# Where the feed-forward stands in the first 18 steps of a top-k attention kernel

## The chip, the cores and the metric

The kernel runs on one core of a Trainium2 chip. A core has TensorE (PE in the profile, with its weight loads as PEld), VectorE (DVE), ScalarE (ACT), GpSimd (POOL) and SyncE (SP), which here issues most of the transfers. Each engine works through its own list of instructions, and they meet through semaphores. The metric is the device time of one execution in microseconds, as the median of several; less is better.

## What is computed

Attention in which each query keeps its 32 largest scores, followed by a feed-forward block with the activation h - tanh(h). The two weight matrices lie in memory as float64, and the kernel converts them; q, k, v and all arithmetic are float32.

```python
B, H, S, D = 8, 8, 576, 64            # q, k, v
scores = np.matmul(q, k.transpose(0, 1, 3, 2)) / np.sqrt(D)
kth = np.partition(scores, -32, axis=-1)[..., -32:-31]
scores = np.where(scores >= kth, scores, -1e9)
attn = np.exp(scores - scores.max(-1, keepdims=True))
attn = attn / (attn.sum(-1, keepdims=True) + 1e-9)
x = (attn @ v).transpose(0, 2, 1, 3).reshape(B * S, H * D)     # 4608 x 512
h = x @ w_in                                                   # 512 x 2048
out = (h - np.tanh(h)) @ w_out                                 # 2048 x 512
```

## The kernel before

The work is a software pipeline over steps. A step is 128 queries of two heads (or the remaining 64 queries of four heads). While step n is searched for its 32 largest values, step n+1 is multiplied, step n-1 is masked and put through the exponential, and step n-2 is turned and multiplied with the values. In the 18 steps of the first batch (`pe` is true) the turning is done by PE, as transposes against an identity, later by DVE and transfers. In the same early steps the 32 pieces of the weights are converted from float64 by DVE, ACT and POOL, two to four pieces a step in steps 0 to 10.

The loop gives each engine its instructions in the order in which they stand here:

```python
for n in range(-4, NS + 4):
    pe = here(-2) and steps[n - 2].pe
    ...
    share, usable = rate(), converted[0]
    if pe:
        w = turn_pe(n - 2)
        next(w)                      # 8 of 9 transposes, 2 copies by ACT
    if here(-1):
        mask(n - 1, exact)           # ACT, POOL
    if here(0):
        search(n, exact, between)    # DVE; the conversion of weights lies in between()
    ...
    if pe:
        spread(n - 2)                # POOL: rx, the divisors
    deal(0.4)
    if here(1):
        scores(n + 1)                # PE, then one copy by ACT
    if pe:
        next(w)                      # the last transpose and its copy
    if here(-1):
        expo(n - 1)                  # ACT
    deal(0.2)
    if pe and steps[n - 2].last:
        values(n - 2)                # PE, ACT, POOL
    deal(0.2)
    for fn in todo.pop(n, []):
        fn()                         # loads
    deal(0.2)
```

`deal` takes items of the feed-forward from a list. A unit of 128 or 256 tokens is put on that list when its last values are done; the first one is, at n = 5. `rate` spreads what is on the list, and what is coming, evenly over the steps.

```python
def deal(part):
    nonlocal credit
    credit += part * share
    while work and credit > 0 and work[0][0] <= usable:
        work.pop(0)[2]()
        credit -= 1
    credit = min(credit, 1.0)
```

An item is one of two things: `ffn_h`, a part of x @ w_in into the tile `hps`, and for every second item a `tanh` and a copy by ACT and a subtraction by POOL; or `ffn_o`, two matmuls of the product with w_out into the tile `ops`, with a copy by ACT after the last part of eight. The profile records each of these float32 matmuls as two instructions.

The functions that the steps speak of, shortened:

```python
def scores(n):
    ps = sc_ps.tile([P, 2, 2, 512], FP32, tag="sc", name="scps")     # one buffer
    ...                                                              # L237: matmuls
    sc = scpool.tile([P, 2, 2, S2], FP32, tag="sc", name="sc")
    nc.scalar.copy(sc[:], ps[:, :, :, 0:S2])                         # L245

def search(n, exact, between):
    ...
    nc.vector.tensor_tensor(lo, ps[:, :, 0, 0:S2], sc[:, :, 1, :], ALU.min)   # L267
    nc.vector.tensor_tensor(hi, ps[:, :, 0, 0:S2], sc[:, :, 1, :], ALU.max)   # L268
    ...                                                              # L270, L275, L278

def mask(n, exact):
    ...                                                              # POOL: tb, nb
    for t in range(2):
        nc.scalar.activation(zv[:, t, :], scf[:, t, :], AF.Relu, ...)          # L307
        nc.gpsimd.tensor_tensor(zv[:, t, :], scf[:, t, :], zv[:, t, :], ALU.subtract)  # L310

def turn_pe(n):
    ...
    for k0 in range(0, KC, J):                                       # KC = 9, J = 4
        zt = zt_ps.tile([P, 512], FP32, tag="zt", name="zt")         # two buffers
        for k in range(kn):
            nc.tensor.transpose(zt[:, ...], z[:, ...], ident[:])     # L409
        nc.scalar.copy(et[:, k0 : k0 + kn], zt[:, ...])              # L412
        if k0:
            yield

def values(n):
    av = zt_ps.tile([P, 2, N], FP32, tag="zt", name="av")            # the same two buffers
    ...                                                              # L433: matmuls of et and v
    nc.tensor.transpose(av[:, 1, ...], rx[:, i], ident[:])           # L441
    nc.scalar.copy(xs[:, :, 0:w], av[:, :, 0:w])                     # L445
    nc.gpsimd.tensor_tensor(xt(u)[...], xv[:, 0], xv[:, 1], ALU.mult)  # L457
    if n in done:
        work.extend(ffn(u))

def convert(piece, slot):                                            # three parts
    ...                                                              # L157, L163: DVE
    nc.scalar.activation(f[:], fu, AF.Relu, bias=e1151[:], scale=-(2.0**23))   # L158
    nc.scalar.activation(e.bitcast(I32), f[:], AF.Relu, bias=e255[:], scale=-1.0)  # L161
    nc.scalar.activation(dst, dst.bitcast(U32), AF.Copy, bias=1.0, scale=2.0**-28) # L166
    yield
    nc.vector.scalar_tensor_tensor(out=fu, in0=hi, ...)              # L169
    nc.gpsimd.tensor_tensor(dst, dst, f[:], ALU.mult)                # L172
```

Of the kernel before, what the change touches and what calls it, by code (L numbers as in the profile page):

```python
# [48 lines left out]
def kernel(  # L49
# [198 lines left out]
    def search(n, exact, between):  # L248

        x = st[n]
        sc, ps = x["sc"], x.pop("ps")
        m = x["m"] = mpool.tile([P, 2, TOP], FP32, tag="m", name="m")
        ab = abpool.tile([P, 2, S + 8], FP32, tag="ab", name="ab")
        if exact:
            cur = [sc[:, t].rearrange("p s k -> p (s k)") for t in range(2)]
            nxt = [ab[:, t, 0:S] for t in range(2)]  # L260
            last = nxt
        else:
            x["ab"] = ab
            cur = nxt = [ab[:, t, 0:S2] for t in range(2)]
            last = [ab[:, t, 0 : S2 + 8] for t in range(2)]
            hi, lo = ab[:, :, 0:S2], ab[:, :, S2 + 8 :]
# [3 lines that stand above are left out]
                nc.vector.max(ab[:, t, S2 : S2 + 8], lo[:, t, :])  # L270
        rounds = TOP // 8
        for i in range(rounds):
            m8 = slice(8 * i, 8 * i + 8)
            for t in range(2):
                nc.vector.max(m[:, t, m8], last[t] if i == rounds - 1 else cur[t])  # L275
            if i < rounds - 1:
                for t in range(2):
                    nc.vector.match_replace(nxt[t], m[:, t, m8], cur[t], NEG)  # L278
                cur = nxt
            between(i)  # L280
# [3 lines left out]
    def mask(n, exact):  # L284

        x = st[n]
        sc, m = x["sc"], x.pop("m")
        scf = sc[:].rearrange("p t s k -> p t (s k)")
        tb = mpool.tile([P, 2], FP32, tag="tb", name="tb")
        if exact:  # L290
            nc.gpsimd.tensor_scalar(tb[:], m[:, :, TOP - 1], BIG, None, ALU.mult)
        else:
            for t in range(2):
                nc.gpsimd.tensor_scalar(  # L294
                    tb[:, t : t + 1],
                    m[:, t, TOP - 1 : TOP],
                    m[:, t, TOP - 9 : TOP - 8],
                    BIG,
                    ALU.min,
                    ALU.mult,  # L300
                )
        nb = mpool.tile([P, 2], FP32, tag="nb", name="nb")
        nc.gpsimd.tensor_scalar(nb[:], m[:, :, 0], -scale, None, ALU.mult)
        z = zpool.tile([P, 2 * S], FP32, tag="z", name="z")
        zv = z[:].rearrange("p (t k) -> p t k", t=2)
        for t in range(2):
            nc.scalar.activation(  # L307
                zv[:, t, :], scf[:, t, :], AF.Relu, bias=tb[:, t : t + 1], scale=-BIG
            )
            nc.gpsimd.tensor_tensor(zv[:, t, :], scf[:, t, :], zv[:, t, :], ALU.subtract)  # L310
        if not exact:
            ab = x.pop("ab")
            for t in range(2):
                nc.gpsimd.tensor_scalar(  # L314
                    bad[:, t, n : n + 1],
                    ab[:, t, S2 + 7 : S2 + 8],
                    BIG,
                    tb[:, t : t + 1],
                    ALU.mult,
                    ALU.is_gt,  # L320
                )
        x.update(z=z, zv=zv, nb=nb)
# [26 lines left out]
    def spread(n):  # L349

        if steps[n].last:
            rd = rds.pop(n)
            nq = steps[n].nq
            rx = rxs[n] = xpool.tile([P, 2, 2, D], FP32, tag="rx", name="rx")
            nc.gpsimd.tensor_copy(
                rx[:, 0:nq], rd[:, 0:nq].unsqueeze(3).to_broadcast([P, nq, 2, D])
            )
# [23 lines left out]
    def spread_keys(n):  # L381


        zx = zxs.pop(n)
        rem = steps[n].rem
        et = ets[n] = et_rem if rem else etpool.tile([P, 4 * S], FP32, tag="et", name="et")
        w = steps[n].nq * S // 2
        for a in range(NG):
            for c in range(NG):
                nc.sync.dma_start(  # L390
                    et[group(c), a * w : (a + 1) * w], zx[group(a), c * w : (c + 1) * w]
                )

    def turn_pe(n):

        g, z = steps[n], st.pop(n)["z"]
        if g.rem:
            et = et_rem
        elif g.i:
            et = ets.pop(n - 1)  # L400
        else:
            et = etpool.tile([P, 4 * S], FP32, tag="et", name="et")[:]
        ets[n] = et
        et = tiles(et, g.nq)[:, :, :, g.i, :].rearrange("p a k j -> p k a j")
        for k0 in range(0, KC, J):
            kn = min(J, KC - k0)
            zt = zt_ps.tile([P, 512], FP32, tag="zt", name="zt")
            for k in range(kn):
                nc.tensor.transpose(  # L409
                    zt[:, k * P : (k + 1) * P], z[:, (k0 + k) * P : (k0 + k + 1) * P], ident[:]  # L410
                )
            nc.scalar.copy(  # L412
                et[:, k0 : k0 + kn],
                zt[:, 0 : kn * P].rearrange("p (k a j) -> p k a j", a=NG, j=G),
            )
            if k0:
                yield
# [152 lines left out]
    def run(exact):  # L570
# [67 lines left out]
        def here(i):  # L638
            return 0 <= n + i < NS

        def between(i):
            for fn in at_round.pop((n, i), []):
                fn()
            if i == 0 and here(-2):
                invert(n - 2)
                if not steps[n - 2].pe:
                    turn_z(n - 2)
# [16 lines left out]
        def rate():  # L664


            have, low, high = len(work), 0.0, None
            coming = sorted((t, u.n // 8) for u, t in ready.items() if t > n)
            for t, k in coming + [(NS + 4, 0)]:
                r = have / max(t - n, 1)  # L670
                high = r if high is None else min(high, r)
                have += k
            for u, t in begun.items():
                if t > n and u in before:
                    need = [i + 1 for i, x in enumerate(work) if x[1] is before[u]]
                    if need:
                        low = max(low, need[-1] / (t - n))
            return max(low, high)
# [3 lines left out]
# [10 lines that stand above are left out]
            if here(-3) and not steps[n - 3].pe:  # L692
                spread(n - 3)
            for m in (n - 4, n - 3):
                if 0 <= m < NS and steps[m].last and steps[m].lag == n - m:
                    values(m)
# [3 lines that stand above are left out]
                next(w)  # L700
            if here(-1):
                mask(n - 1, exact)
            if here(0):
                search(n, exact, between)
            elif here(-2):
                between(0)
            if here(-2) and not pe and steps[n - 2].last:
                spread_keys(n - 2)
            if pe:
                spread(n - 2)  # L710
            deal(0.4)
            if here(1):
                scores(n + 1)
            if pe:
                next(w)
            if here(-1):
                expo(n - 1)
            deal(0.2)
            if pe and steps[n - 2].last:
                values(n - 2)  # L720
            deal(0.2)
            for fn in todo.pop(n, []):
                fn()
            deal(0.2)
# [4 lines left out]
    with tc.manual_schedule():  # L729
        run(False)  # L730
# [10 lines left out]
    with tc.If(again > 0):  # L741
        with tc.manual_schedule():
            run(True)
# [29 lines left out]
```

## Time and profile before

| | before |
|---|---|
| time, median of 3 runs | 1548.89 us (1547.83 to 1551.28) |
| span of the profiled run | 1548.3 us, 25298 instructions |
| PE busy | 1440.6 us, 93% |
| DVE busy | 1347.3 us, 87% |
| POOL busy | 941.5 us, 61% |
| ACT busy | 883.4 us, 57% |
| shares of the chain that ended last | PE 73%, DVE 9%, others 5% or less each |

The busy share is a mean over the whole span, and the kernel has parts with different limits; so the page is read with the forty slices beside the totals, and then the trace by step. A busy PE is a modelled thing, as the ends of matmuls are. In the list of waits a line names who waited, for whom, how long in total, how often and the longest. A releaser in brackets behind an instruction is who ended the idle time before it. A row of the timeline merges like instructions that follow each other.

Two waits stand large over the whole span and have to do with the steady part, not with the first 18 steps: in 300 to 1500 us ScalarE waits 147.7 us for the values of PE at line 445, and GpSimd 146.4 us for ScalarE at line 457. In that stretch PE is busy 99 to 100% from 400 us on, so they cost nothing there.

### The profile page before, as it was taken

The page shows a single profiled execution, that of the slowest core. Times are in us where ns is not written, and L with a number is a line of the kernel's source. Part 1 is how long each engine was busy: PE and PEld are TensorE (multiplying, and loading weights), DVE is VectorE, ACT ScalarE, POOL GpSimd, SP SyncE. Part 2 cuts the span into 40 slices and gives each one's busy share as a digit, 9 for nine tenths or more (in the row PEclk, how much of TensorE's full clock was granted, in tenths as well). Part 3 has the DMA queues.
Part 4 walks back from the last instruction along what each step waited for, and adds up shares of the span by engine and source line. Part 5 has one row for each costly group of instructions (what it writes and reads, how often), then busy time and mean ns, then how long its engine had stood idle before and what let it go on. Part 6 is the DMA issues. An engine that isn't in the chain of part 4 may idle for free.

```text
span 1548.3 us, 25298 instructions
## 1 busy us (share of the span) xinstructions
PE 1440.6 (93%) x7428; PEld 912.4 (59%) x7428; DVE 1347.3 (87%) x3828; ACT 883.4 (57%) x1567; POOL 941.5 (61%) x1525
## 2 busy tenths in 40 slices
PE   2467899999999999999999999999999999999997
PEld 1355466556565665656566665656566665656673
DVE  6997889999999999999999999999999999997300
ACT  4886767556565565656565565656565565655320
POOL 2776567667565675757575675757565675746420
PEclk9787899999999999999999999999999999999999
DMA  9954113334443354234433354234443345322200
GB/s 233 364 182 155 50 25 66 85 77 88 112 92 76 82 105 104 70 77 96 106 88 78 81 107 102 70 79 97 101 90 80 80 99 110 81 64 59 73 10 16
DMA packets 258835, 147.42 MB, mean 95 GB/s; under 512 B 210048, under 2 KB 217216, under 8 KB 258688
## 3 DMA queue, kind: packets, MB, share of 16 engines
q1 hardware_dynamic: 256912, 145.49, 38.6%
q8 instruction: 62, 1.02, 0.3%
q14 instruction: 85, 0.70, 0.2%
q10 hardware_dynamic: 1776, 0.22, 0.1%
HBM read 61.85 MB, written 9.44 MB: 46 GB/s over the span
## 4 chain that ended last, share of the span: by engine, by line
PE 73%; DVE 9%; SPq 5%; ACT 4%; DMA 3%; issue 3%; POOL 2%; DVEq 0%; ACTq 0%; POOLq 0%
PE hps L486 27%; PE ops L507 27%; PE av L433 9%; PE scps L237 8%; SPq L390 4%; DVE ab L278 3%; DVE m L275 3%; PE av L441 2%; SPq L200 1%; DMA zx<-in_moe_w_in_dram 1%; DVE spare L376 1%; DVE ab L270 1%; DVE ab L267 1%; DVE ab L268 1%; ACT sc L245 1%
## 5 line engine op out<-in xcount | busy, mean ns | idle before, releaser
L507 PE MATMUL ops<-w_out,g 128*128 128x512 f32 x1152 | 524.1, 601 | 0.0
L486 PE MATMUL hps<-xT,w_in 128*128 128x256 f32 (+1 forms) x2176 | 473.8, 373 | 1.2 <-POOL xT L457 1.2
L275 DVE MAX8 m<-ab 128x8 f32<-128x288 f32 (+1 forms) x1152 | 463.4, 443 | 0.0
L310 POOL TENSOR_TENSOR z<-sc,z 128x576 f32<-128x576 f32 x288 | 400.1, 1411 | 82.3 <-ACT z L307 82.3
L486 PEld LDWEIGHTS hps<-xT,w_in 128*128 128x128 f32 x2176 | 392.4, 193 | 73.4 <-issue 24.4
L278 DVE MATCH_REPLACE8 ab<-m,ab 128x288 f32<-128x288 f32 x864 | 375.5, 442 | 0.0
L507 PEld LDWEIGHTS ops<-w_out,g 128*128 128x128 f32 x1152 | 211.4, 191 | 243.0 <-issue 239.4
L307 ACT ACTIVATE z<-sc,tb 128x576 f32<-128x576 f32 x288 | 207.6, 769 | 154.0 <-POOL tb L294 154.0
L500 POOL TENSOR_TENSOR g<-g,th 128x512 f32<-128x512 f32 x144 | 184.0, 1278 | 123.0 <-ACT g L499 112.9
L245 ACT COPY sc<-scps 128x1152 f32<-128x1152 f32 x144 | 161.0, 1118 | 114.3 <-PE scps L237 110.4
L330 ACT ACTIVATE z<-z,nb 128x576 f32<-128x576 f32 x288 | 221.5, 773 | 7.1 <-POOL z L310 7.0
L237 PE MATMUL scps<-kT,qT 64*128 64x288 f32 (+1 forms) x1280 | 184.5, 437 | 30.7 <-DVE qT L222 28.5
L433 PE MATMUL av<-et,vb 128*64 128x256 f32 (+1 forms) x1088 | 132.9, 379 | 43.8 <-ACT et L412 37.7
L237 PEld LDWEIGHTS scps<-kT,qT 64*128 64x128 f32 (+1 forms) x1280 | 100.1, 181 | 122.9 <-issue 60.0
L267 DVE TENSOR_TENSOR ab<-scps,sc 128x576 f32<-128x576 f32 x144 | 107.6, 747 | 70.1 <-POOL bad L314 58.2
L498 ACT ACTIVATE th<-hps 128x512 f32<-128x512 f32 x144 | 85.4, 593 | 107.8 <-PE hps L486 105.4
L457 POOL TENSOR_TENSOR xT<-xs 128x256 f32<-128x256 f32 (+1 forms) x68 | 47.3, 695 | 160.7 <-ACT xs L445 160.6
L445 ACT COPY xs<-av 128x512 f32<-128x512 f32 (+1 forms) x84 | 44.2, 526 | 163.6 <-PE av L441 163.4
L433 PEld LDWEIGHTS av<-et,vb 128*64 128x64 f32 x1088 | 75.5, 139 | 102.9 <-ACT et L412 39.6
L340 POOL TENSOR_SCALAR rd<-den 128x2 f32<-128x2 f32 x144 | 33.4, 232 | 145.4 <-ACT z L330 100.3
L270 DVE MAX8 ab<-ab 128x8 f32<-128x288 f32 x288 | 116.4, 445 | 0.0
L268 DVE TENSOR_TENSOR ab<-scps,sc 128x576 f32<-128x576 f32 x144 | 107.4, 746 | 0.0
(67 smaller groups left out, 1249.0 us busy)
## 6 DMA issues: line engine op xcount, KB each, us to landing
et<-spare SPq DMA_DIRECT2D x448, 72.0 KB, 2.0
et<-zx SPq DMA_DIRECT2D x448, 72.0 KB, 2.0
kin<-in_k_dram SPq DMA_DIRECT2D x116, 72.0 KB, 2.3
vb<-in_v_dram SPq DMA_DIRECT2D x64, 128.0 KB, 2.5
out_dram<-ot SPq DMA_DIRECT2D x32, 256.0 KB, 2.2
qin<-in_q_dram SPq DMA_DIRECT2D x113, 72.0 KB, 2.3
w_out<-in_moe_w_in_dram SPq DMA_DIRECT2D x10, 512.0 KB, 5.7
w_out<-in_moe_w_in_dram SPq DMA_DIRECT2D x10, 511.5 KB, 6.3
```

The lines of the kernel that those rows point to most:

```text
L237: nc.tensor.matmul(ps[rows, t, s, 0:S2], qT[g.b, g.hp + i][half(t), qs], kT[g.b, g.hp + i][half(t), ks], start=True, stop=True,)
L245: nc.scalar.copy(sc[:], ps[:, :, :, 0:S2])
L270: nc.vector.max(ab[:, t, S2 : S2 + 8], lo[:, t, :])
L275: nc.vector.max(m[:, t, m8], last[t] if i == rounds - 1 else cur[t])
L278: nc.vector.match_replace(nxt[t], m[:, t, m8], cur[t], NEG)
L307: nc.scalar.activation(zv[:, t, :], scf[:, t, :], AF.Relu, bias=tb[:, t : t + 1], scale=-BIG)
L310: nc.gpsimd.tensor_tensor(zv[:, t, :], scf[:, t, :], zv[:, t, :], ALU.subtract)
L330: nc.scalar.activation(x["zv"][:, t, :], x["zv"][:, t, :], AF.Exp, bias=x["nb"][:, t : t + 1], scale=scale, accum_out=den[:, t : t + 1],)
L433: nc.tensor.matmul(av[half(t), 0, cols], vb[g.b, hp][:, t, c, :] if c < J else vr[g.b, hp][:, t, :], es[:, :, (J + 1) * t + c if c < J els ...
L486: nc.tensor.matmul(cur[u][:, s : s + w], w_in[j][:, c, fo : fo + P], u.xT[:, c, 0:w], start=(c == 0), stop=(c == CD - 1),)
L500: nc.gpsimd.tensor_tensor(g, g, th[:], ALU.subtract)
L507: nc.tensor.matmul(cur[u][:], u.g[o // 1024][:, o % 1024 // 512, o % 512 : o % 512 + P], w_out[f // FJ][:, f % FJ, :], start=(f == 0), sto ...
```

## The change

In a step in which PE does the turning, nothing of the feed-forward is dealt ahead of the scores any more; four fifths of the step's share are dealt between the last transpose and the values, and one fifth at the end of the step. The other steps deal as before. It is meant to give the next step's scores to ScalarE and VectorE sooner and to give PE work where the values wait for the copy of the last transpose.

```diff
             if pe:
                 spread(n - 2)
-            deal(0.4)
+            deal(0.0 if pe else 0.4)
             if here(1):
                 scores(n + 1)
             if pe:
                 next(w)
             if here(-1):
                 expo(n - 1)
-            deal(0.2)
+            deal(0.8 if pe else 0.2)
             if pe and steps[n - 2].last:
                 values(n - 2)
-            deal(0.2)
+            deal(0.0 if pe else 0.2)
             for fn in todo.pop(n, []):
                 fn()
             deal(0.2)
```

## The prediction

> **What bounds the kernel now.** I read the slices of the page first, to see where TensorE (PE) is not full. These are its lines for PE, VectorE (DVE) and the granted clock, 38.7 us to a digit:
>
> ```profile
> PE   2467899999999999999999999999999999999997
> ...
> DVE  6997889999999999999999999999999999997300
> ...
> PEclk9787899999999999999999999999999999999999
> ```
>
> From the sixth slice on PE is full and sets the end; only the first five or six slices leave it idle, at a lower clock. Those are the first 18 steps, the ones that the change touches. PE's whole work is the same before and after, so the change can only pay by making this head shorter. What it gains there should reach the end, because everything after the head is the same list of work.
>
> Second, the busy time by step. I took the start of the line 267 minimum as the start of a step. Steps 6 to 10 and, for contrast, step 12 (columns: stretch, length, then busy us of PE, weight loads, DVE, ScalarE (ACT), GpSimd (POOL), clock, DMA):
>
> ```profile
> 88.04:101.02 12.98, 11.11 (x76) 9.49 (x76) 12.85 (x35) 11.94 (x24) 9.42 (x13) 0.78 0.27 95
> 101.02:115.59 14.57, 7.23 (x64) 6.26 (x64) 12.88 (x36) 12.19 (x24) 11.71 (x15) 0.95 0.62 214
> 115.59:131.76 16.17, 12.00 (x86) 10.64 (x86) 12.85 (x34) 12.01 (x24) 12.15 (x15) 0.82 0.40 135
> 131.76:148.89 17.13, 11.14 (x63) 8.66 (x64) 12.75 (x35) 12.81 (x25) 12.06 (x15) 0.70 0.49 172
> 148.89:169.47 20.58, 12.26 (x38) 5.71 (x35) 14.22 (x37) 12.92 (x24) 10.96 (x14) 0.75 0.30 103
> ...
> 177.88:186.98 9.10, 9.10 (x55) 5.70 (x51) 7.61 (x25) 6.99 (x15) 5.07 (x9) 1.00 0.14 39
> ```
>
> Step 6 is as long as its DVE work (12.85 of 12.98). Steps 7 to 10 have nearly the same DVE work, but take 14.57 to 20.58 us: here nothing is full, so a chain across engines sets the pace. From step 12 PE is full. Steps 2 to 5 (37.46 to 88.04) have no feed-forward yet, and cannot change.
>
> Third, the timeline of PE in step 8, to find that chain (start, duration, line, form, idle before it and its releaser):
>
> ```profile
> 115.97 0.42 PE L433 MATMUL av<-et,vb 128*64 128x128 f32 x1
> 117.36 3.62 PE L486 MATMUL hps<-xT,w_in 128*128 128x128 f32 x16
> 120.78 1.18 PE L409 MATMUL zt<-ident,z 128*128 128x128 f32 x8
> 121.79 1.95 PE L486 MATMUL hps<-xT,w_in 128*128 128x128 f32 x16
> 123.67 1.24 PE L237 MATMUL scps<-kT,qT 64*128 64x288 f32 x8
> 125.01 1.95 PE L486 MATMUL hps<-xT,w_in 128*128 128x128 f32 x16
> 131.88 0.48 PE L433 MATMUL av<-et,vb 128*64 128x128 f32 x1 [3.90 <-ACT et L412]
> ```
>
> The reader is to see a loop. PE stands 3.90 us in the values for the last `et` copy (line 412) of ACT. Released, it first does one feed-forward item, cold (3.62 us), and only then the transposes (120.78) for which ACT stands in turn:
>
> ```profile
> 121.61 1.07 ACT L412 COPY et<-zt 128x512 f32<-128x512 f32 x2 [3.63 <-PE zt L409]
> 122.57 1.45 ACT L307 ACTIVATE z<-sc,tb 128x576 f32<-128x576 f32 x2
> 123.91 0.72 ACT L158 ACTIVATE f<-f,e 128x512 f32<-128x512 uint32 x1
> ...
> 129.59 0.58 ACT L498 ACTIVATE th<-hps 128x512 f32<-128x512 f32 x1
> 130.07 0.57 ACT L499 COPY g<-hps 128x512 f32<-128x512 f32 x1
> 130.53 1.13 ACT L245 COPY sc<-scps 128x1152 f32<-128x1152 f32 x1
> 131.54 0.29 ACT L412 COPY et<-zt 128x128 f32<-128x128 f32 x1
> ```
>
> ACT has 10.2 us of its own in order (121.61 to 131.83) before it releases PE. PE's part, 131.88 to ACT's next copies at 138.22 in the same timeline, is about 6.3. Sum 16.5; the step took 16.17, and the copies came 16.61 apart (121.61 to 138.22): this is the loop. DVE stands inside it, at the weight conversion. The waits of 90 to 200 us say the same:
>
> ```profile
> PE av L433 <- ACT et L412: 16.9, 4, 5.7
> DVE f L169 <- ACT f L161: 14.3, 4, 5.3
> ACT et L412 <- PE zt L409: 12.7, 9, 3.9
> ```
>
> **What the Trainium skill says.** "TensorE: Matmul & The Clock Gate", Part 1: after an idle window of about 3.4 us the clock falls to half. The trace agrees: the same 16 matmuls take 1.95 us in a run of work and 3.62 us after waits of 5.69 and 3.90. "Perfetto Trace Analysis", Tensor Engine Instruction: ACT and DVE take their queues strictly in order, and PE reorders only weight loads. The timeline agrees: at 115.37 ACT's 0.28 us `et` copy comes after nine conversion operations, a `tanh` and two copies, although its transpose was ready at 109. So where work stands in program order is what counts here, and that is all the change alters. The same page, Optimization Strategy, says that the most-contended engine may change between regimes; the step table shows it (DVE, then the loop, then PE).
>
> **The change part by part.** No instruction is removed or added. The shares dealt per step sum to 1.0 before and after, and the rule takes items until the credit is used, so each step deals as many items as before. From the code I get a share of about 2.4 items a step from step 6 to 18; the PE timeline shows 3, 2, 3, 2, 3 in steps 6 to 10. An item is 16 recorded matmuls of line 486 or 4 of line 507, 1.9 us warm. Before, usually one item stood ahead of the scores, none or one behind the last transpose, and one after the values. After: following the credit by hand (0.8 of 2.4 is 1.9 a step), two items stand between the last transpose and the values in each step, and a third after the values only in steps 6, 8, 10, 13, 15 and so on; none ahead of the scores.
>
> What this does to the loop:
> 1. **Ahead of the scores**, ACT's `tanh` and copy leave the path to the score copy: 130.53 minus 129.59 is 0.94 us. ACT's part falls from 10.2 to 9.3 us. They move to after the exponentials, where ACT had idle time.
> 2. **Before the values**, two items of 1.95 us, partly cold, fill the wait of 3.9 to 5.7 us. They should end before the `et` copy is there, so they cost nothing.
> 3. **After the values**, the item goes in two steps of three or every second one: 3.62 us less before the transposes. Where one stays, it is likely warm, 1.95.
> PE's part is then about 1.2 us of values, 0.3 of transposes of the divisors and 0.9 of transposes, 2.4, or 4.4 with an item. But ACT itself has two exponentials (1.95 us with their sums, 131.70 to 133.35 in the same timeline), `tanh` and copy (about 1.05) and `xs` (0.37), together 3.4, before its next copies. The loop is 9.3 plus 3.4 to 4.5, or **12.7 to 13.8 us**. DVE's own 12.75 to 12.88 then bounds or nearly bounds.
>
> By step:
> - Step 6 stays 12.98, DVE being full. Its third item still follows the values, so step 7 starts its transposes as late as before (104.75) and keeps its DVE wait of 1.49; it gains about 0.2.
> - Step 8: 16.17 to 13.0 (12.85 of DVE and a small wait), gain 3.2.
> - Step 9: its transposes follow an item, DVE waits some 0.7: 17.13 to 13.5, gain 3.6.
> - Step 10 converts four pieces: 14.22 of DVE, plus the DMA waits that the DVE timeline shows (0.28 and 0.74; a landing of a reused buffer, which don't move), plus 0.4: 15.6 instead of 20.58, gain 5.0.
> Sum 12.0. From step 11 PE is full and its work is the same. There are 1.3 and 0.24 us of idle PE in steps 14 and 15 (9.20 of 10.50, 9.14 of 9.38), and a cold item in step 11 (3.62 for 1.88, but some other work will be cold in its stead). Scores that come one item sooner help DVE, which is full from 214 us. I put 1.4 us for all that. Total 13.4: 1548.9 minus 13.4 is **1535.5 us**.
>
> **The rivals.** First, the head is bound by DVE, and then nothing comes of it. For: DVE is 85 to 99% busy there in most steps. Against: its waits in steps 7 to 10 sum to 14.3 on line 169 alone. Time then: 1547 to 1549. Second, a new wait takes the place of the old one: scores that stand directly behind the transposes meet a score buffer that DVE has not yet read (one buffer), the last transpose meets a `zt` buffer (two) that ACT has not copied, or the two items run cold (7.2 us) and delay the values. In step 8 the transposes would end near 118.3 and DVE has read the scores by 117; two cold items would still end about when the `et` copy comes. So I expect small waits, not the old ones; if the rival is right half the gain goes, 1541 to 1544. Third, the head gets shorter and it is lost again in the full part, as DVE is full from 214 to 400 us and PE from there. Both start sooner with the same lists, so I see no cause; time then about 1548. Fourth, the gain is larger: all DVE waits of steps 7 to 10 (68.45 us of steps against 52.7 of DVE work, so 15.75) and some 3 us of PE waits go, 1530.
>
> **Range and chances.** The fourth rival gives the lower end, 1529.5; half of my gain, with a little for the 3.5 us spread of the runs before, the upper end, 1543.5. Faster by over 2% needs 31 us, which isn't idle in this stretch: 0.01. A loss of 31 us would need a new wait of 2 us in every changed step: 0.01. Within 2%: 0.98, most of it on the faster side.
>
> **What would show it.** In the changed kernel: steps 8, 9 and 10 at about 13, 13.5 and 15.6 us with DVE work unchanged; `PE av <- ACT et` from 16.9 to some 6 us in total; `DVE f <- ACT f` from 14.3 to under 4; the 3.62 us cold items after the values gone; step 11 starting near 157.5 instead of 169.5 and the step at 214.4 near 201; the same PE work after. It would be wrong if PE waits at the scores for DVE's reading, if ACT's `tanh` and copies now delay `xs` and with it the second half of the transposes by more than the item that went, or if the head's gain is not found at the end.

## The result, and the profile after

The changed kernel takes **1544.22 us** (median of 6 runs, 1542.66 to 1545.55) where the kernel before takes 1549.22 (6 runs). The ratio is 0.9963, with a 95% interval of 0.995 to 0.9975: 5.0 us less, clear of the spread, but not the 13.4 us of the prediction, and 0.7 us above its range. The slices of the page, for PE, DVE and the granted clock, hardly differ from those of before:

```profile
PE   2567899999999999999999999999999999999997
...
DVE  6998899999999999999999999999999999997300
...
PEclk9887999999999999999999999999999999999999
```

The gain is all in the head. Step 6 begins 0.38 us sooner than before (87.66 to 88.04; the steps before it have the same work in both), step 11 4.85 us sooner (164.62 to 169.47), step 16 5.52 us sooner (208.92 to 214.44). From there to the end both traces take the same: 1333.88 us after, 1333.86 before. So what the head gains is kept, and the question is only why steps 7 to 10 gave 4.47 us (68.45 to 63.98) instead of the expected 12.0. The busy time by step, after, for steps 6 to 10 (columns as in the prediction):

```profile
87.66:100.64 12.98, 10.72 (x76) 8.64 (x76) 12.86 (x34) 11.93 (x24) 9.42 (x13) 0.81 0.30 93
100.64:116.57 15.93, 11.24 (x86) 10.05 (x86) 12.80 (x36) 11.91 (x23) 11.65 (x14) 0.89 0.56 198
116.57:130.34 13.77, 10.21 (x71) 8.21 (x70) 12.83 (x35) 12.21 (x24) 11.66 (x14) 0.75 0.43 148
130.34:147.74 17.40, 11.93 (x62) 8.67 (x62) 12.78 (x35) 13.06 (x26) 12.11 (x15) 0.79 0.49 177
147.74:164.62 16.88, 10.41 (x34) 5.42 (x31) 14.14 (x37) 12.76 (x24) 10.96 (x14) 0.80 0.36 126
```

Steps 8 and 10 got shorter (16.17 to 13.77, 20.58 to 16.88); steps 7 and 9 got longer (14.57 to 15.93, 17.13 to 17.40). DVE's work is what it was. Steps 7 and 9 are the ones that follow a step with an item behind the values. PE's timeline from the values of step 7 to the transposes of step 9 shows both kinds:

```profile
115.98 0.32 PE L433 MATMUL av<-et,vb 128*64 128x128 f32 x1 [2.92 <-ACT et L412]
...
118.35 0.47 PE L441 MATMUL av<-ident,rx 128*128 128x128 f32 x1 [1.70 <-POOL rx L355]
118.61 1.91 PE L409 MATMUL zt<-ident,z 128*128 128x128 f32 x8
120.46 2.29 PE L237 MATMUL scps<-kT,qT 64*128 64x288 f32 x8
122.68 0.47 PE L409 MATMUL zt<-ident,z 128*128 128x128 f32 x1
122.95 3.91 PE L486 MATMUL hps<-xT,w_in 128*128 128x128 f32 x32
...
129.74 0.32 PE L433 MATMUL av<-et,vb 128*64 128x128 f32 x1 [1.86 <-ACT et L412]
...
132.10 0.48 PE L441 MATMUL av<-ident,rx 128*128 128x128 f32 x1 [1.59 <-POOL rx L355]
132.37 3.62 PE L486 MATMUL hps<-xT,w_in 128*128 128x128 f32 x16
135.79 1.62 PE L409 MATMUL zt<-ident,z 128*128 128x128 f32 x8
```

The two items before the values (32 recorded matmuls at 122.95) stand where the prediction had them, and the wait for the last `et` copy falls from 3.90 to 1.86 us. Two things stand behind it that the prediction did not have: PE waits 1.70 and 1.59 us for `rx`, GpSimd's copy of the divisors, and the item at 132.37 is still cold, 3.62 us, at a granted clock of 0.50 (130.14 to 136.97). On ScalarE that item has a second effect:

```profile
136.09 0.60 ACT L498 ACTIVATE th<-hps 128x512 f32<-128x512 f32 x1 [3.10 <-PE hps L486]
136.59 0.58 ACT L499 COPY g<-hps 128x512 f32<-128x512 f32 x1
137.05 1.09 ACT L412 COPY et<-zt 128x512 f32<-128x512 f32 x2
```

Its `tanh` and copy stand ahead of the `et` copies of the next transposes. The waits of 90 to 200 us, after:

```profile
DVE f L169 <- ACT f L161: 11.0, 4, 4.6
PE av L433 <- ACT et L412: 10.7, 4, 3.9
...
ACT et L412 <- PE zt L409: 6.8, 10, 3.5
...
PE av L441 <- POOL rx L355: 6.3, 4, 1.8
```

The first three fell from 14.3, 16.9 and 12.7; the last one rose, from 3.6 over the same stretch.

### The profile page after: what moved, and what is told of

Read it like the earlier page. It is cut to its first block, busy times and chain, and to the rows that moved or that the text cites. A ratio compares the mean times of both kernels' runs of the same rounds, so it can differ in the third digit from the quotient of the medians.

```text
span 1542.8 us, 25300 instructions
## 1 busy us (share of the span) xinstructions
PE 1440.7 (93%) x7428; PEld 912.1 (59%) x7428; DVE 1347.2 (87%) x3828; ACT 883.9 (57%) x1567; POOL 940.8 (61%) x1525
## 4 chain that ended last, share of the span: by engine, by line
PE 73%; DVE 10%; SPq 5%; ACT 4%; DMA 2%; issue 2%; POOL 2%; DVEq 0%; ACTq 0%; POOLq 0%
PE ops L507 28%; PE hps L486 26%; PE av L433 9%; PE scps L237 8%; SPq L390 3%; DVE m L275 2%; DVE ab L278 2%; PE av L441 2%; SPq L200 2%; DMA zx<-in_moe_w_in_dram 1%; DVE spare L376 1%; PE zt L409 1%; DVE ab L267 1%; DVE ab L270 1%; DVE ab L268 1%
## 5 line engine op out<-in xcount | busy, mean ns | idle before, releaser
L237 PE MATMUL scps<-kT,qT 64*128 64x288 f32 (+1 forms) x1280 | 188.1, 445 | 31.7 <-DVE qT L222 28.1
```

The costliest lines, as they stand in the source:

```text
L237: nc.tensor.matmul(ps[rows, t, s, 0:S2], qT[g.b, g.hp + i][half(t), qs], kT[g.b, g.hp + i][half(t), ks], start=True, stop=True,)
```

## The experiments

Eight kernels, each against the kernel before on the same chip (1548.78 us in the first four runs, 1550.27 in the others, so ratios are compared rather than times). Each kernel has one trace. Length of the steps from the starts of line 267 in each trace:

| kernel | step 7 | step 8 | step 9 | step 10 | sum | time | ratio and interval |
|---|---|---|---|---|---|---|---|
| before | 14.57 | 16.17 | 17.13 | 20.58 | 68.45 | 1549.22 | 1 |
| changed | 15.93 | 13.77 | 17.40 | 16.88 | 63.98 | 1544.22 | 0.9963 [0.995, 0.9975] |
| none after the values | 13.76 | 13.78 | 15.14 | 16.98 | 59.66 | 1538.30 | 0.9926 [0.991, 0.9943] |
| early rx | 13.36 | 14.16 | 15.40 | 15.74 | 58.66 | 1537.18 | 0.9922 [0.9907, 0.9938] |
| both of these | 13.36 | 14.17 | 14.95 | 15.73 | 58.21 | 1535.65 | 0.991 [0.9893, 0.9926] |
| first half of the change | 14.29 | 16.25 | 17.40 | 20.14 | 68.08 | 1549.92 | 1.0004 [0.9996, 1.0013] |
| second half of the change | 17.06 | 14.35 | 16.23 | 17.00 | 64.64 | 1545.86 | 0.996 [0.9944, 0.9975] |
| an item doubled | 15.83 | 13.78 | 15.63 | 17.22 | 62.46 | 1543.83 | 0.9949 [0.9934, 0.9964] |
| both, tanh put off | 13.35 | 14.17 | 14.73 | 15.74 | 57.99 | 1538.77 | 0.9916 [0.99, 0.9932] |
| before, with early rx | 13.63 | 15.97 | 15.93 | 18.29 | 63.82 | 1544.75 | 0.9956 [0.994, 0.9972] |

**None after the values.** The changed kernel, with the whole share before the values:

```diff
-            deal(0.8 if pe else 0.2)
+            deal(1.0 if pe else 0.2)
...
-            deal(0.2)
+            deal(0.0 if pe else 0.2)
```

> Change: the changed kernel, with the whole share dealt between the last transpose and the values and none at the end of the step. In the changed kernel steps 7 and 9 follow a step with an item after the values and take 15.93 and 17.40 us; steps 8 and 10 follow one without and take 13.77 and 16.88. Theory A (an item between the values and the next transposes is on the loop, and costs 3.4 to 3.6 us there because TensorE is cold, plus its tanh and copy): steps 7 and 9 fall to about 13.8 each, steps 8 and 10 stay, so 5.7 us less than the changed kernel, about 1538.5. Rival B (three items before the values make the values late): steps 7 and 9 fall by at most 2 us in all, the wait for the last et copy vanishes, time 1542 to 1544. Rival C (the divisors' copy on GpSimd holds the step whatever stands after the values): steps 7 and 9 don't fall below 15.

1538.30 us, 4.3 us less in steps 7 to 10 than the changed kernel. Step 7 falls to 13.76 as expected, step 9 only to 15.14. Steps 8 and 10 stay. Three items before the values still leave PE waiting for the `et` copy (0.91 us in step 8), so they don't make the values late. Theory A holds for step 7 to a tenth; step 9 stays above 15 us, as rival C had it, and there PE still waits 1.72 us for `rx`.

**Early rx.** The changed kernel, with GpSimd's copy of the divisors ahead of the later weight conversions:

```diff
             if i == 0 and here(-2):
                 invert(n - 2)
+                if steps[n - 2].pe:
+                    spread(n - 2)
...
-            if pe:
-                spread(n - 2)
```

> Change: the changed kernel, with GpSimd's copy of the divisors (rx) given right after VectorE's reciprocal in the first round of the search, ahead of the later weight conversions, instead of behind them. In the changed kernel TensorE waits 1.80, 1.70, 1.59 and 1.24 us for it in steps 6 to 9. Theory (this wait took the place of part of the one removed, and lies on the loop): the waits go, TensorE is perhaps warmer, steps 7 to 10 get shorter by about 1.2 us each, in all 4 to 6 us, 1538.5 to 1540. Rival (the wait is hidden behind ScalarE, which has exponentials, tanh and copies to do until then): under 1.5 us in all, 1543 to 1544.

1537.18 us. Steps 7 to 10 are 5.3 us shorter, and steps 3 to 5, which have no feed-forward, 35.45 instead of 37.11 us. So the rival falls: this wait was on the loop. PE's timeline of this kernel in steps 6 and 8 shows it gone, and the items behind the values shorter:

```profile
96.89 0.33 PE L441 MATMUL av<-ident,rx 128*128 128x128 f32 x1
97.06 1.95 PE L486 MATMUL hps<-xT,w_in 128*128 128x128 f32 x16
...
125.09 0.48 PE L441 MATMUL av<-ident,rx 128*128 128x128 f32 x1
125.36 2.85 PE L486 MATMUL hps<-xT,w_in 128*128 128x128 f32 x16
```

1.95 and 2.85 us instead of 3.38 and 3.62. Two costs went at once here, the wait and part of the slow clock behind it. Step 8 is 0.4 us longer than in the changed kernel: ScalarE waits there 1.33 us for GpSimd's thresholds (`tb`), 0.26 in the changed kernel.

**Both.** The two edits together:

> Change: both of the above, no item after the values and the early copy of the divisors. If both costs lie on the loop and VectorE is the next bound (12.8 us of work in steps 7 to 9, 14.2 and about one of waiting for a landing in step 10): steps 7, 8, 9 at 13.0 to 13.3 and step 10 at 15.5, 1535 to 1537, which is what the prediction had for the change. If VectorE isn't the next bound, steps of 13.8, 1538.

1535.65 us, the time that the prediction had for the change, and the lowest median here, though the intervals of the next ones overlap with it. But the steps are 13.36, 14.17, 14.95 and 15.73, not 13.0 to 13.3 in the first three: the two edits overlap, and the second adds 1.5 us to the first, within the intervals. The trace shows what stands in step 9 now. With three items in a step ScalarE may have two `tanh` and two copies ahead of `xs`, and the second half of the transposes needs the buffer that `xs` frees; then GpSimd has two subtractions ahead of the thresholds. First PE, then ScalarE, in that step:

```profile
128.65 0.66 PE L409 MATMUL zt<-ident,z 128*128 128x128 f32 x4 [2.31 <-ACT xs L445]
```

```profile
131.56 1.44 ACT L307 ACTIVATE z<-sc,tb 128x576 f32<-128x576 f32 x2 [1.62 <-POOL tb L294]
```

**The first half of the change.** Nothing ahead of the scores, but 0.4 behind the values as before:

```diff
-            deal(0.8 if pe else 0.2)
+            deal(0.6 if pe else 0.2)
...
-            deal(0.0 if pe else 0.2)
+            deal(0.2 if pe else 0.2)
```

> Change: one half of the change alone. Nothing ahead of the scores, but 0.6 of the share before the values and 0.4 after them as before, so about one item after the values in each step. Theory A (the item after the values is what counts): hardly better than the kernel before, 1547 to 1549, with steps 8 and 9 at 16 to 17 us. Rival (what pays is that the scores and their copy come sooner and that the wait before the values is filled): most of the gain, 1544 to 1546.

1549.92 us, no gain at all, as theory A had it. In steps 7 to 10 the loop is as long as ever:

```profile
113.30:129.55 16.25, 12.07 (x90) 10.48 (x87) 12.82 (x35) 12.00 (x24) 11.64 (x14) 0.82 0.38 135
129.55:146.95 17.40, 10.19 (x58) 7.96 (x58) 12.79 (x35) 13.07 (x26) 12.11 (x15) 0.70 0.46 169
146.95:167.09 20.14, 12.29 (x38) 5.84 (x35) 14.14 (x37) 12.80 (x24) 10.97 (x14) 0.75 0.30 105
```

**The second half of the change.** 0.4 stays ahead of the scores, and 0.4 before the values, 0.2 at the end:

```diff
-            deal(0.0 if pe else 0.4)
+            deal(0.4 if pe else 0.4)
...
-            deal(0.8 if pe else 0.2)
+            deal(0.4 if pe else 0.2)
```

> Change: the other half of the change alone. 0.4 of the share stays ahead of the scores, 0.4 stands before the values, none directly after them and 0.2 at the end of the step: one item ahead of the scores, one or none before the values, and one after them only in every second step. The first half alone gave nothing (1549.92 us). Theory A (only what stands between the values and the next transposes counts): nearly the whole gain of the changed kernel, 1543 to 1546, with steps 8 and 10 near 14 to 15 and 17 to 18 us and steps 7 and 9 near 15 to 17. Rival (the two halves need each other: with an item ahead of the scores, its tanh stands ahead of the score copy, and PE reaches the values late): 1547 to 1549.

Ratio 0.996, the whole gain. So the first part of the change, none ahead of the scores, does nothing to the time that can be measured; what pays is that fewer items stand between the values and the next transposes.

**An item doubled.** The changed kernel, in which the first item before the values is multiplied twice in steps 6 and 8:

```diff
+        twice = again.pop() if again else 1
...
+            for _ in range(twice):
+                for c in range(CD):
...
+            if n in (6, 8):
+                again.append(2)
             deal(0.8 if pe else 0.2)
+            again.clear()
```

> Change: the changed kernel, in which TensorE multiplies the first item before the values twice in steps 6 and 8 (the product is written anew, so the output is the same; 16 recorded matmuls more in each). It fills TensorE's waits of 2.08 and 1.86 us for the last et copy, ahead of the items after the values that took 3.38 and 3.62 us. Theory A (those items were slow because TensorE had been idle before them, and their length lies on the loop): with more work they take 1.95 to 2.9 us, steps 7 and 9 get 0.7 to 1.5 us shorter each, and the kernel with more work is faster, 1541.5 to 1543.5. Rival (the clock doesn't follow the short waits, or the length of the item is hidden): same time or up to 1 us slower, 1544 to 1545.5.

Step 9 falls from 17.40 to 15.63 us, with more work on PE. In step 8 the item behind the values is warm now, although the wait for `rx` is as long as in the changed kernel:

```profile
132.13 0.33 PE L441 MATMUL av<-ident,rx 128*128 128x128 f32 x1 [1.72 <-POOL rx L355]
132.29 1.95 PE L490 MATMUL hps<-xT,w_in 128*128 128x128 f32 x16
```

1.67 us shorter item, 1.77 us shorter step: its length lies on the loop. That its slowness came of PE's idle time before it, the granted clock bears out: it is 0.50 from 130.14 to 136.97 us in the changed kernel, and 1.00 from 123.87 to 144.35 here. In step 6 the item only fell from 3.38 to 2.97, and step 7 from 15.93 to 15.83: there the clock still fell to 0.50, at 103.39, 0.70 us after the item's start. The time as a whole can't be told from that of the changed kernel (0.9949 and 0.9963, the intervals overlap), so the effect is read from the steps of one trace alone.

**Both, with the tanh put off.** In the kernel with both edits, ScalarE's `tanh` and copy and GpSimd's subtraction (`rest` in the cut) follow the values:

```diff
+            if held[0]:
+                put_off.append(rest)
...
             if pe and steps[n - 2].last:
                 values(n - 2)
+            for fn in put_off:
+                fn()
+            put_off.clear()
             deal(0.0 if pe else 0.2)
```

> Change: the kernel with both earlier changes (no item after the values, early copy of the divisors; 1535.65 us), in which ScalarE's tanh and copy and GpSimd's subtraction for the items before the values are given after the values, so that xs and xT come first. In that kernel TensorE waits 2.31 us for xs in step 9, with two tanh and two copies ahead of it on ScalarE, and ScalarE waits 1.62 us for GpSimd's thresholds behind two subtractions. Theory (xs behind the feed-forward on ScalarE is what keeps step 9 at 14.95 us): the waits for xs fall under 1 us, steps 8 and 9 get 0.5 to 1 us shorter each, 1534 to 1535. Rival (ScalarE has that work to do before the next copies wherever it stands): no change, 1535.5.

The waits for `xs` fall to 0.7 us in all, but step 9 gives only 0.22 us and step 8 nothing: the rival is right, ScalarE does that work ahead of the next copies wherever it stands (in step 9 they start 3.58 us after the copy that released PE, in both kernels). The edit leaves the subtractions ahead of the thresholds on GpSimd, and ScalarE's wait for these in step 9 is 1.76 us where it was 1.62; this wait is untested. Step 14 pays 2.6 us for it (9.53 to 12.17), where VectorE now waits 4.52 us for GpSimd's last reading of its buffer. The ratio, 0.9916, is no better than 0.991.

**Before, with early rx.** The same early copy in the kernel before:

> Change: the kernel before, with only the early copy of the divisors. There TensorE waits 1.79, 0.27, 0.28 and 1.23 us for it in steps 6 to 9. If that wait only took the place of the one that the change removed, little comes of it here: 1.7 us in steps 3 to 5, which have no feed-forward and got that much shorter in the changed kernel with the early copy, and at most 1 us later, so 1546 to 1547.5. Rival (the copy costs its whole length whatever stands around it, 7 us as in the changed kernel): 1542.

A miss, and the rival came true: 1544.75 us, ratio 0.9956. The expected 1546 to 1547.5 us would be 0.998 to 0.999 of the 1549 they start from, outside the interval; the rival's 1542 would be 0.9955. The early copy brings the kernel before as much as the change does. Of that 4.6 us are in steps 7 to 10 (68.45 to 63.82) and 1.4 in steps 3 to 5 (37.09 to 35.69). The wait for `rx` did not take the place of another; it cost as much before, though I had read only 0.27 and 0.28 us of it in steps 7 and 8. Steps 9 and 10 gain most, 1.2 and 2.3 us, and in step 9 part of that is the clock: the item behind the values of step 8 takes 2.75 us instead of 3.62. The two gains add: 0.9963 times 0.9956 is 0.9919, and the changed kernel with the early copy measured 0.9922.

## Why the prediction was wrong, point by point

**Right.** The head is the place, and the loop of values, transposes, copies and conversions is the mechanism: its length by its own terms is the step, before and after. After step 7, ScalarE's copies came 3.85 us after the copy that released PE (115.92 to 119.77), and ScalarE's own part was 9.93 (to 129.70); 13.78, for a step of 13.77, at the upper end of the 12.7 to 13.8 predicted. The count and place of items, the unchanged DVE work, the gain kept to the end, and the two items before the values that cost nothing held too. One reading was off without harm: the two exponentials from 131.70 to 133.35 take 1.65 us, not 1.95 (their records overlap), so the lower end of the loop was 12.4, not 12.7.

The signs show how far it fell short: `PE av <- ACT et` went to 10.7 us and not to some 6, `DVE f <- ACT f` to 11.0 and not under 4, and step 11 starts at 164.62 and not near 157.5.

**Wrong, first: "Where one stays, it is likely warm, 1.95."** It took 3.38 us in step 6, where it had taken 1.95 before, and 3.62 in step 8. In step 6 this is nearly the whole error: step 7 was put at 14.4 and took 15.93, and the item was 1.43 us too long. I had taken the filled wait for a continuous run of PE. What was left, 2.08 and 1.80 us before the one item, 1.86 and 1.59 before the other, was enough to slow them: the granted clock is 0.50 from 102.83 to 106.25 and from 130.14 to 136.97. The doubled item shows the cause for step 8; in step 6 the doubled item still left the stretch ahead of the fall (99.98 to 103.39) with 1.54 us of PE work, and the clock fell (last section).

**Wrong, second: "PE's part is then about 1.2 us of values, 0.3 of transposes of the divisors and 0.9 of transposes, 2.4, or 4.4 with an item."** The sum has no term for `rx`. The copy stood in the queue of GpSimd behind the third weight conversion, 1.24 to 1.80 us too late in steps 6 to 9. Without an item ScalarE's exponentials hide part of it; with one they don't. Step 8 to 9 in the same terms: copies 7.35 us after the releasing copy (129.70 to 137.05) where the sum had 4.4. The cold item is 1.67 of the difference and `rx` 1.59, 3.26 together against 2.95. ScalarE's part was 10.07 where the prediction had 9.3, 0.69 of it a wait for GpSimd's thresholds. 17.42 in all, against 13.7.

**Wrong, third: "ACT's `tanh` and copy leave the path ... 0.94 us"** as a gain. It is true of the place (9.23 us from copies to copy in step 7, 10.2 before), but the first half of the change shows that this is worth nothing while an item stays behind the values.

**The rivals.** The second one, that a new wait takes the place of the old one, had nearly the right size, 1541 to 1544, by luck, as it gave other reasons: neither the score buffer nor the `zt` buffer held the loop, and the items before the values were not late. What held it stood after the values. Step 10, put at 15.6, took 16.88; with the early copy it took 15.74. The 1.4 us for steps 11 to 16 were 0.67.

The kernel with both edits puts the sum to the test: it removes the two terms that were missing, and its steps 7 to 10 last 58.21 us where the prediction had 56.5: of the 7.5 us that the change fell short of in these steps (12.0 expected, 4.47 measured) the two give back 5.8. That its time, 1535.65 us, is the predicted 1535.5 is in part luck: steps 3 to 5, which the prediction held fixed, gave 1.3 us (37.09 to 35.80) toward the 1.7 that these steps fell short.

## What to carry to other kernels

When a loop across engines sets the pace, list every instruction between one release and the next on each engine in queue order, also the small copies (here 0.29 us on GpSimd) that stand behind others' work; the wait they cause is hidden in one version and bare in the next. Work that one moves off such a loop pays only if nothing stays in its place: half the items behind the values left half the cost. And count on a slow TensorE after waits; one warm item in one trace doesn't show that the next run has it warm (next section).

## What the runs showed that I had not expected

Two short waits can slow TensorE as one long one does: after 2.08 and 1.80 us, with 0.65 us of values between them (99.96 to 100.61), sixteen matmuls took 3.38 us, while after 1.70 and 1.79 in the kernel before they took 1.95. The granted clock tells the cases apart. In each trace it changes only at the edges of a grid of 3.41 us, and from one trace to the next the grid lies elsewhere. Cut along it, the changed kernel shows this ahead of the two cold items (after the length, the first figure is PE's busy time; the clock is the third from the end):

```profile
99.42:102.83 3.41, 1.07 (x10) 0.83 (x11) 3.41 (x7) 3.02 (x9) 2.56 (x5) 1.00 0.99 335
102.83:106.25 3.42, 3.42 (x19) 3.42 (x18) 3.42 (x13) 0.32 (x1) 3.19 (x5) 0.50 0.88 332
...
126.73:130.14 3.41, 1.55 (x22) 1.24 (x20) 3.41 (x9) 3.38 (x6) 2.21 (x2) 1.00 0.89 309
130.14:133.55 3.41, 1.82 (x11) 1.46 (x9) 3.41 (x10) 2.41 (x7) 2.83 (x4) 0.50 0.99 354
```

The kernel before, in step 6, and the doubled item, in step 8, both keep the full clock:

```profile
97.16:100.58 3.42, 1.72 (x23) 1.36 (x22) 3.42 (x10) 3.39 (x7) 2.47 (x2) 1.00 0.87 310
100.58:103.99 3.41, 1.62 (x17) 1.38 (x14) 3.41 (x9) 2.57 (x7) 2.59 (x4) 1.00 0.97 348
103.99:107.40 3.41, 3.41 (x33) 3.39 (x31) 3.41 (x14) 1.96 (x4) 2.54 (x6) 1.00 0.65 261
```

```profile
127.28:130.70 3.42, 3.13 (x35) 2.71 (x34) 3.42 (x8) 3.41 (x7) 1.82 (x3) 1.00 0.94 357
130.70:134.11 3.41, 1.98 (x18) 1.98 (x19) 3.41 (x11) 1.86 (x5) 3.24 (x5) 1.00 1.01 345
```

In the ten traces, from the first record of the clock (44 to 58 us) to 300 us, every such stretch at full clock with under 1.5 us of PE work (77 of them) is followed by one at half, and every one with over 1.7 us (492) by one at full; between these figures (13) both occur. So the warm item of step 6 in the kernel before was partly luck: its two waits fell into different stretches, while an equal stretch from 99.80 to 103.21 us would have held 1.07 us of work. For the doubled item the place of the grid isn't the reason: the same stretch of the changed kernel, 127.29 to 130.70, holds 1.36 us.

The Trainium skill, "TensorE: Matmul & The Clock Gate", Part 1, says that the activity is watched in windows of about 3.4 us that run freely, and the grid in these traces agrees. It also says that an idle window brings the clock to half; here a window with 1.55 us of work did so as well (126.73 to 130.14), and the measurement decides.

In such a loop more matmul work in a wait can make the step shorter: 16 recorded matmuls more in step 8, and step 9 1.77 us less.
